# Linear attention and a gated convolution FFN on one core: PSUM handed out in single banks, with a new order

## The chip, the core and the metric

The kernel runs on one core of one Trainium2 chip. Its engines work side by side and wait for each other through semaphores: TensorE (PE in the profile; its weight loads are shown apart as PEld), VectorE (DVE), ScalarE (ACT), GpSimd (POOL, which here issues the loads that cast from fp32 to bf16) and SyncE (SP, which issues the stores). TensorE writes its results to PSUM, an accumulator of 128 partitions and eight banks; a bank holds 512 fp32 numbers per partition. DVE and ACT read PSUM and write SBUF.

The metric is the time of one execution on the device in microseconds (us), median of the runs shown. The kernel before takes 180.43 us (three runs, 179.78 to 180.63).

## The reference

There are 8 batches, 8 heads, 576 tokens and 64 numbers per head; the model width is 8 x 64 = 512, and the FFN is 1024 wide.

```
kv  = einsum('bhsd,bhse->bhde', k, v)          # linear attention, no softmax
out = einsum('bhsd,bhde->bhse', q, kv)
x   = out / sqrt(mean(out*out, -1) + 1e-6) * g_norm      # per head, then heads side by side
h   = maximum(x @ w_in, 0)
c   = conv_w[0]*h[t-1] + conv_w[1]*h[t] + conv_w[2]*h[t+1]
y   = (h * sigmoid(c)) @ w_out                  # float32, 8 x 576 x 512
```

## The kernel before

**An order written out.** The body defines small operations, one Python function each (decorated with `op`). A long string, ORDER, names them one after the other, and the kernel records them in that order; at the end a dependency is added between neighbours of each engine, so every engine executes its own instructions in the order of the string. A token such as `hm.0.4.0@3` means operation `hm` with arguments 0, 4, 0, and the number behind `@` names the buffers that it opens. A letter behind `!` is the engine that does an eviction: A for ACT, V for DVE. Nothing is scheduled at run time: where an instruction waits, all behind it on its engine wait too.

**PSUM before.** All accumulators come from one pool with four tags `a0` to `a3`, each of 1024 fp32 columns, so two banks. `tl` opens a tile in a tag; the next tile in that tag waits until every reader of the last one is done, even if it needs one bank alone.

**The stages**, with the operations that the prediction speaks of:

- Loads: `Lq`, `Lk`, `Lv` load a batch of q, k or v, often in halves (two of the four head groups), into two buffers per tensor; `Li` and `Lo` load the weights. All are on POOL's queue, in the order of the string (L358, L372, L377). A load waits until the batch before the last has been used up. The first halves of batch 0 come through SP instead and are cast by `ca`.
- Attention per batch b and half u: `qt` transposes q (36 small matmuls, L422) and `qc` copies the result to SBUF (qT); `kv` multiplies k by v (36 small matmuls, L397) and `kvc` copies it (kvw); `ot` makes the outputs of two head groups (L443).
- Norm of batches 0 and 1: `sq` squares, `on` sums over each head (L432, L433), `nl` takes the reciprocal root on ACT (L465), and `mz` writes the normed x (xT) on DVE (L472). Of batches 2 to 7, in pairs: `sq`, `oc` (copy of the output to SBUF), `ss` (sums), `ln`, `sl` (four DVE instructions that split the root into two parts, L501 to L504), `sp` (spreads it over the partitions, L513) and `mu` (DVE, L520). `sl.3` belongs to the third pair, batches 6 and 7.
- First projection: for batches 0, 1, 6 and 7 `hm` in two steps of two contractions (L536, 288 columns each) and `re` for the relu. For the pairs of batches (2, 3) and (4, 5), 1152 tokens long, `ha.p.f.e` makes 512 tokens (e = 0, 1) of feature block f (L549); `rea` is their relu, over 1024 columns at once; `hb` and `reb` do the last 128 tokens.
- Convolution and gate: `ta` (two multiplications by a tap, L585 and L586), `aa` and `ab` (sums, L592 and L598) on DVE, `sg` (sigmoid, ACT, L630), `mg` (product of gate and h, DVE, L636).
- Second projection: `om.p.k.i` makes group k of the output tiles of pair p with half i of the eight contraction blocks; a group is two tiles of 128 tokens (two banks) or one. i = 0 and i = 1 are placed on their own, and either may come first. `ea` copies the group to SBUF (a row buffer, one of four), and `st` stores it. The very last tile (3, 6) is done in two halves of 256 columns.
- Fillers: `fi`, `fn`, `fq`, `fo` are matmuls on zeros that nobody reads. They stand in the first 35 us, where PE would have nothing to do.

`sw` ties the next store to a load: the store waits until that load has landed.

The lines that say how a tile of PSUM is opened and how the groups of the second projection are evicted:

Of the kernel before, what the change touches and what calls it, by code (L numbers as in the profile page):

```python
# [66 lines left out]
STORES2 = [(0, 1), (0, 2), (0, 0), (0, 3)]  # L67
# [8 lines left out]
Li.0 mz.0.0 sq.0.2@2 qc.1.0!V@2 fn.2.128.on.0.2@3 on.0.2 sq.0.3@3 nl.0.2@1 mz.0.2 on.0.3@1 nl.0.3 mz.0.3 hm.0.4.0@3
hm.0.5.0@1 hm.0.1.0@2 hm.0.5.1 hm.0.4.1 Li.3 hm.0.1.1 hm.0.0.0@0 re.0.5!A@1 ta.0.5@0 re.0.4!A ta.0.4 hm.0.0.1 aa.0.2
re.0.1!A re.0.0!A Lq.1.1 ab.0.2 qt.1.1@1 hm.0.7.0@3 sg.0.4 Lk.1.0@1 hm.0.6.0@2 Lv.1.0@1 Li.1 ta.0.1@1 hm.0.6.1
re.0.6!A ta.0.0 kv.1.0@0 kvc.1.0!V hm.0.7.1 qc.1.1!V@3 Lv.1.1 ot.1.0@0,2 hm.0.2.0@1 hm.0.2.1 sg.0.5 aa.0.0 re.0.7!A
sq.1.0@4 ab.0.0 sq.1.1@5 sg.0.1 hm.0.3.0@3 re.0.2!V sg.0.0 hm.0.3.1 Lk.1.1 Lq.2.0@0 mg.0.2 re.0.3!V fq.1.512.kv.1.1@1  # L80
kv.1.1 kvc.1.1!V Lk.2.0@0 fo.2.384.1.0 on.1.1@3 nl.1.1@2 ta.0.7@0 on.1.0@1 ta.0.6 mg.0.0 Lv.2.0@0 fo.5.384.1.0
qt.2.0@3 mz.1.1 nl.1.0 qc.2.0!A@4 fq.1.512.ot.1.1@1 fq.1.256.ot.1.1 ot.1.1@2 sq.1.3@6 mz.1.0 Lq.3.1@1 aa.0.3
fo.2.384.1.2 kv.2.0@3 on.1.3@0 Lq.2.1 sq.1.2@7 kvc.2.0!A fo.2.384.1.3 on.1.2@3 nl.1.3@3 nl.1.2 fo.1.384.1.2 hm.1.6.0@0
ab.0.3 hm.1.4.0@3 ta.0.2@1 mz.1.3 mz.1.2 fi.2.512@2 hm.1.4.1 sg.0.7 re.1.4!A hm.1.6.1 Lq.3.0 ta.0.3 qt.2.1@2 re.1.6!A
aa.0.1 Lv.3.1@1 qt.3.0@1 qt.3.1@3 ab.0.1 hm.1.7.0@0 hm.1.7.1 Lk.3.1@1 sg.0.6 Lk.2.1 sg.0.3 qc.3.0!V@0 qc.3.1!V@1
sg.0.2 hm.1.0.0@1 re.1.7!A qc.2.1!V@2 hm.1.0.1 mg.0.3 ta.1.6@0 ta.1.7 ot.2.0@3,2 re.1.0!A oc.2.1@4 sq.2.1@0 Lv.2.1
Lo.0 hm.1.2.0@0 hm.1.2.1 oc.2.0 sq.2.0@1 mg.0.1 aa.1.3 hm.1.5.0@1 hm.1.5.1 re.1.2!A hm.1.3.0@2 hm.1.3.1 re.1.5!A
ta.1.4@1 kv.2.1@3 re.1.3!A kv.3.1@0 ab.1.3 kvc.2.1!V Lo.1 hm.1.1.0@1 ot.2.1@3,2 ta.1.5 sg.1.6 Lk.3.0 kvc.3.1!V sg.1.7
aa.1.2 ab.1.2 oc.2.2@0 hm.1.1.1 sq.2.2@2 Lv.3.0 om.0.1.0@0 re.1.1!V sg.1.5 ot.3.1@3,1 Lq.4.1@0 sq.2.3@3 Lq.5.0@1
mg.1.3 ta.1.0@0 ta.1.1 sg.1.4 oc.2.3 mg.1.2 om.0.1.1 aa.1.0 ta.1.2@1 oc.3.3@1 sq.3.2@5 om.0.0.0@2 sq.3.3@4 kv.3.0@1  # L90
oc.3.2 ab.1.0 ta.1.3 kvc.3.0!V qt.4.1@3 ea.0.1!A@0 aa.1.1 sg.1.1 qc.4.1!V@3 ab.1.1 sg.1.0 mg.1.0 ot.3.0@0,1 om.0.0.1
om.0.2.1@3 ea.0.0!V@1 sq.3.0@6 sq.3.1@7 ss.2@2 ss.3 sg.1.2 sg.1.3 mg.1.1 ln.1@0 Lv.5.1@0 sl.1@0 oc.3.0@2 Lk.5.0@0
# [24 lines left out]
sg.3.4 re.6.0!A sg.3.5 ta.4.6@0 hm.7.0.0@3 hm.6.5.1 re.6.5!A hm.7.0.1 re.7.3!V ta.4.7 hm.7.6.0@1 hm.6.3.0@2 hm.7.6.1
aa.4.3 ab.4.3 st.1.0 hm.6.3.1 hm.7.2.0@0 re.7.6!A mg.3.2 sg.4.7 re.7.0!A hm.7.2.1 re.7.2!A om.2.4.0@1 ta.4.5@1 ta.4.4
aa.4.2 ab.4.2 sg.4.6 hm.7.1.0@3 om.2.4.1 ea.2.4!A@0 sg.4.5 sg.4.4 re.6.3!A mg.4.3 ta.5.7@0 ta.5.6 aa.5.3 ab.5.3 mg.4.2
ta.4.2@1 ta.4.3 aa.4.1 sg.5.6 hm.6.1.0@0 hm.6.1.1 sg.5.7 mg.5.3 ab.4.1 hm.7.1.1 re.6.1!A ta.4.1@0 sg.4.3 ta.4.0  # L120
om.2.0.0@1 om.2.0.1 om.2.1.1@2 om.2.1.0 ea.2.0!A@1 sg.4.2 st.1.1 aa.4.0 ab.4.0 om.2.3.1@0 om.2.2.1@1 sg.4.0 sg.4.1
st.2.0 om.2.3.0 mg.4.1 ea.2.1!A@2 ta.5.4@1 mg.4.0 ta.5.3@0 ta.5.5 aa.5.2 ta.5.2 ab.5.2 om.3.1.0@2 aa.5.1 ea.2.3!A@3
sg.5.5 om.3.0.0@0 om.3.0.1 re.7.1!V om.3.1.1 ab.5.1 sg.5.4 mg.5.2 sg.5.2 st.2.1 st.2.3 ea.3.0!A@1 st.3.0 ta.5.0@1
ea.3.1!A@2 ta.5.1 aa.5.0 ab.5.0 sg.5.0 om.3.2.1@3 om.2.2.0 sg.5.1 mg.5.0 st.3.1 sg.5.3 om.3.5.1@0 om.3.3.1@2
ea.2.2!A@3 st.2.2 mg.5.1 om.3.3.0 om.3.2.0 st.2.4 om.3.4.0@1 ea.3.2!V@1 ea.3.3!A@2 st.3.3 om.3.5.0 ea.3.5!A@3 st.3.2
om.3.6.1@2 st.3.5 ea.3.6.1!A@0 st.3.6.1 om.3.4.1 ea.3.4!A@2 st.3.4 om.3.6.0 ea.3.6.0!A@1 st.3.6.0
"""


@with_exitstack  # L130
def kernel(
    ctx: ExitStack,
    tc: tile.TileContext,
    q: bass.AP,
    k: bass.AP,
    v: bass.AP,
    g_norm: bass.AP,
    moe_w_in: bass.AP,
# [20 lines left out]
    work = pool("work", 1)  # L159
    psum = pool("psum", 1, space=PSUM)  # L160

    T = {}
    ops = {}
    slots = []

    def tl(key, r, shape, dtype, name):
        if key not in T:
            s = slots.pop(0)
            kw = {}
            if r == "a":  # L170
                n = 1
# [115 lines left out]
    def first_tile(name, *a):  # L287
        if name == "ot":
            b, j = a
            return tl(("ot", b, 2 * j if b in JOINT else j), "a", [P, 1024], FP32, "o_ps")  # L290
# [445 lines left out]
```

## Time and profile before

| | us |
|---|---|
| median of three runs | 180.43 (179.78 to 180.63) |
| profiled execution | 180.49 |
| its span, first to last instruction | 178.7 |
| PE busy | 169.0 |
| DVE busy | 151.5 |
| ACT busy | 143.4 |
| POOL busy | 34.7 |
| ACT, output copies (row) of 1024 and 512 columns | 13 of 1.030, 6 of 0.594 |
| ACT, relu of 1024 and 512 columns | 13 of 1.030, 2 of 0.612 |
| DVE, relu of 1024 and 512 columns | 3 of 1.221, 2 of 0.684 |

The last three rows are mean durations of one instruction. Instructions overlap at their ends: a duration is longer than the step from one start to the next. The chain of work that ended last counts such steps, so the prediction takes its prices from there. The profiled execution's own time is 1.8 us longer than its span, for what lies before the first instruction and behind the last. A busy PE need not be a productive one: zeros for nobody count as busy, and matmuls overlap, so columns per time are the better measure.

### The profile page before, as it was taken

Reading aid. Unit: us, or ns where it says so; the run is one execution under the profiler, and the core shown is the slowest. Engines: PE = TensorE matmul, PEld = TensorE weight load, DVE = VectorE, ACT = ScalarE, POOL = GpSimd, SP = SyncE. Lnnn points to the kernel's source line nnn. Section 1 sums busy time; section 2 is a strip of 40 time slices with the busy share of each in tenths; the row PEclk is TensorE's granted clock in tenths of the full one; section 3 lists DMA queues with packets and bytes.
Section 4 is the critical chain, followed back from the end, with each engine's and each line's share of the span. In section 5 each row is a group of like instructions: output and inputs, shape, how many; then the busy total and the mean of one; then the engine's idle time right before and its main releaser. Section 6 shows DMA issues by size and latency. Waiting matters only on the chain.

```text
span 178.7 us, 5121 instructions
## 1 busy us (share of the span) xinstructions
PE 169.0 (95%) x2206; PEld 91.3 (51%) x2206; DVE 151.5 (85%) x271; ACT 143.4 (80%) x200; POOL 34.7 (19%) x60
## 2 busy tenths in 40 slices
PE   7898998999999989989999999999999999999992
PEld 2344754577444454544454474343478764444451
DVE  2467699999997794999999999999999999999410
ACT  2575699999999647979998999999479984757832
POOL 6954536441643022400000000000000000000000
PEclk9999999999999999999999999999999999999999
DMA  5999999999999999999970000001075000242674
GB/s 196 357 200 198 204 207 205 207 205 207 208 206 207 209 226 152 206 185 254 172 269 6 0 6 0 0 4 59 0 274 201 0 0 0 94 189 72 235 293 176
DMA packets 21354, 27.21 MB, mean 152 GB/s; under 512 B 1224, under 2 KB 15828, under 8 KB 21332
## 3 DMA queue, kind: packets, MB, share of 16 engines
q0 software_dynamic: 15072, 15.09, 51.5%
q1 hardware_dynamic: 6256, 11.80, 17.7%
q8 instruction: 17, 0.28, 0.6%
q14 instruction: 5, 0.04, 0.1%
q10 hardware_dynamic: 4, 0.00, 0.0%
HBM read 32.52 MB, written 9.44 MB: 235 GB/s over the span
## 4 chain that ended last, share of the span: by engine, by line
PE 37%; ACT 29%; DVE 21%; DMA 5%; issue 4%; POOL 2%; POOLq 0%; ACTq 0%
PE om_ps L655 22%; PE h_ps L536 10%; ACT taps L630 8%; ACT h L228 7%; DMA q_sb<-in_q_dram 5%; ACT sq L450 5%; ACT o L222 4%; DVE xT L520 3%; DVE taps L585 3%; DVE taps L586 3%; DVE taps L598 2%; DVE taps L592 2%; ACT L217 2%; DVE h L636 2%; DVE h L230 1%
## 5 line engine op out<-in xcount | busy, mean ns | idle before, releaser
L655 PE MATMUL om_ps<-w_out_sb,h 128*128 128x512 bf16 x280 | 63.5, 379 | 0.3 <-DVE xT L520 0.3
L630 ACT ACTIVATE taps<-taps,cw 128x576 bf16<-128x576 bf16 (+1 forms) x48 | 43.9, 956 | 6.4 <-DVE taps L598 6.2
L655 PEld LDWEIGHTS <-h 128*128 128x128 bf16 x280 | 26.6, 98 | 31.9 <-issue 2.1
L536 PE MATMUL h_ps<-xT,w_in_sb 128*128 128x288 bf16 x256 | 33.8, 286 | 0.4 <-ACT o L465 0.2
L228 ACT ACTIVATE h<-h_ps 128x576 bf16<-128x576 f32 (+2 forms) x42 | 30.6, 770 | 3.7 <-PE h_ps L536 3.5
L549 PE MATMUL h_ps<-xT,w_in_sb 128*128 128x512 bf16 x128 | 29.7, 380 | 0.0
L536 PEld LDWEIGHTS <-w_in_sb 128*128 128x128 bf16 x256 | 24.6, 98 | 8.9 <-issue 2.0
L222 ACT ACTIVATE row<-om_ps 128x1024 f32<-128x1024 f32 (+2 forms) x21 | 17.7, 844 | 12.1 <-PE om_ps L655 9.2
L636 DVE TENSOR_TENSOR h<-h,taps 128x1152 bf16<-128x1152 bf16 (+1 forms) x24 | 22.7, 951 | 1.9 <-ACT taps L630 1.8
L598 DVE TENSOR_TENSOR taps<-taps,h 128x1152 bf16<-128x1152 bf16 (+1 forms) x24 | 22.9, 954 | 0.6
L592 DVE TENSOR_TENSOR taps<-taps 128x1152 bf16<-128x1152 bf16 (+1 forms) x24 | 23.0, 956 | 0.4
L450 ACT ACTIVATE sq<-o_ps 128x576 bf16<-128x576 f32 x32 | 20.5, 680 | 2.7 <-PE o_ps L443 2.7
L585 DVE TENSOR_SCALAR taps<-h,cw 128x576 bf16<-128x576 bf16 (+1 forms) x48 | 20.8, 434 | 1.8 <-ACT h L228 1.8
L586 DVE TENSOR_SCALAR taps<-h,cw 128x576 bf16<-128x576 bf16 (+1 forms) x48 | 20.4, 425 | 0.0
L520 DVE SCALAR_TENSOR_TENSOR xT<-o,cw,sp_ps 128x576 bf16<-128x576 f32 x24 | 18.1, 809 | 1.3 <-PE sp_ps L513 1.3
L549 PEld LDWEIGHTS <-w_in_sb 128*128 128x128 bf16 x128 | 11.7, 98 | 14.2 <-issue 1.4
L222 ACT ACTIVATE o<-o_ps 128x576 f32<-128x576 f32 x24 | 15.5, 677 | 1.0 <-ACT o L222 0.8
L358 POOL DMA_DIRECT2D v_sb<-in_v_dram x13 | 9.4, 720 | 18.6 <-PE kv_ps L397 13.3
L358 POOL DMA_DIRECT2D q_sb<-in_q_dram x13 | 9.4, 721 | 14.8 <-PE qt_ps L422 11.0
L217 ACT ACT_TABLE_LOAD x8 | 10.3, 1283 | 2.1 <-issue 2.0
L230 DVE TENSOR_SCALAR h<-h_ps 128x576 bf16<-128x576 f32 (+2 forms) x10 | 8.8, 878 | 2.4 <-PE h_ps L549 2.4
L358 POOL DMA_DIRECT2D k_sb<-in_k_dram x12 | 8.7, 724 | 3.6 <-PE kv_ps L397 1.7
(78 smaller groups left out, 138.2 us busy)
## 6 DMA issues: line engine op xcount, KB each, us to landing
out_dram<-row SPq DMA_DIRECT2D x10, 512.0 KB, 2.8
out_dram<-row SPq DMA_DIRECT2D x15, 256.0 KB, 3.0
q_sb<-in_q_dram POOLq DMA_DIRECT2D x11, 288.0 KB, 11.1
v_sb<-in_v_dram POOLq DMA_DIRECT2D x11, 288.0 KB, 10.9
k_sb<-in_k_dram POOLq DMA_DIRECT2D x10, 288.0 KB, 10.8
stg<-in_k_dram SPq DMA_DIRECT2D x2, 576.0 KB, 6.0
q_sb<-in_q_dram POOLq DMA_DIRECT2D x2, 576.0 KB, 10.2
v_sb<-in_v_dram POOLq DMA_DIRECT2D x2, 576.0 KB, 10.1
```

The costliest lines, as they stand in the source:

```text
L222: nc.scalar.activation(to, fr, AX.Copy)
L228: nc.scalar.activation(to, fr, AX.Relu)
L358: loads[x, b] = nc.gpsimd.dma_start(out=qkv(x, b)[:, w0:w0 + n, :], in_=rows(x, b, w0, n))
L450: nc.scalar.activation(by_r(s), natural(T["ot", b, t][:, :S]), AX.Square)
L536: nc.tensor.matmul(ps[:, e, :HS], w_in_sb[:, t, f * P:(f + 1) * P], x[:, t, e * HS:(e + 1) * HS], start=(t == 0), stop=(t == NT - 1))
L549: nc.tensor.matmul(ps[:, e], w_in_sb[:, t, f * P:(f + 1) * P], x[:, t, e * 512:(e + 1) * 512], start=(t == 0), stop=(t == NT - 1))
L585: nc.vector.tensor_scalar_mul(tap[:, 0, f % 2, :n, 8:8 + S], h[:, f], cw[:, f:f + 1])
L592: nc.vector.tensor_add(tap[:, 1, :, :n, :S], tap[:, 0, :, :n, 7:7 + S], tap[:, 1, :, :n, 1:1 + S])
L598: nc.vector.tensor_add(y, y, h[:, 2 * j:2 * j + 2])
L630: nc.scalar.activation(y, y, AX.Sigmoid, scale=scale)
L636: nc.vector.tensor_mul(h, h, T["tap", c, j][:, 1, :, :n, :S])
L655: nc.tensor.matmul(ps[:, j], h[:, f, m * P:(m + 1) * P], w_out_sb[:, f, :], start=first and f == 4 * i, stop=not first and f == 4 * i + 3)
```

## The change

PSUM becomes one tile of eight banks, and a number in the order is now a bank, 0 to 7. An accumulator that needs two banks takes the named one and its neighbour; one that needs one bank takes that alone. Dependencies follow the columns that are written and read.

Two things are done in smaller pieces. `ha` opens one bank for each 512 tokens, and `rea` has an instruction for each (32 in place of 16). `om` makes one output tile of 128 tokens at a time (a fourth argument j), in a bank of its own, and `ea` copies that tile alone; the store still takes the whole group. The number of matmuls that compute something is the same. The fillers name a bank in place of an accumulator.

The order is new from the second token on. The loads have other places in POOL's queue; some evictions are on another engine than before; the fillers are other ones (36 and 20 of 128 columns in place of nine and six of 512 at the start, for instance). Operations that the order did not use (`cd`, `cp`, `fn`) are gone. STORES2, which says which groups are stored in two pieces, lists the same four in another sequence.

```diff
-STORES2 = [(0, 1), (0, 2), (0, 0), (0, 3)]
+STORES2 = [(0, 0), (0, 3), (0, 2), (0, 1)]
...
-pre@0,0,0 ca.q.1!V ca.q.0!A fi.9.512@1 fi.1.128@1 qt.0.0@0 pn Lq.0.1 ca.k.1!V qc.0.0!A@0 Lv.0.1 ca.k.0!V fi.6.512@2
...
-ea.2.2!A@3 st.2.2 mg.5.1 om.3.3.0 om.3.2.0 st.2.4 om.3.4.0@1 ea.3.2!V@1 ea.3.3!A@2 st.3.3 om.3.5.0 ea.3.5!A@3 st.3.2
-om.3.6.1@2 st.3.5 ea.3.6.1!A@0 st.3.6.1 om.3.4.1 ea.3.4!A@2 st.3.4 om.3.6.0 ea.3.6.0!A@1 st.3.6.0
+pre@0,0,0 Lq.0.1 ca.q.0!V ca.q.1!V fi.36.128@0 fi.3.128@0 qt.0.0@0 qc.0.0!V@0 fi.1.512@2 fi.20.128@2 ct@0 ca.k.1!V
...
+om.3.1.1.0 om.3.0.1.1 ea.3.1.0!V sg.5.1 ea.3.0.1!V sg.5.3 mg.5.1 st.3.1 om.3.3.1@2 om.3.4.1@0 sg.5.0 st.3.0 om.3.2.1@1
+mg.5.0 ea.2.0.1!V st.2.0 om.3.4.0 ea.3.4!A@1 om.3.2.0 om.3.5.0 ea.3.2!V@3 om.3.3.0 st.3.4 st.3.2 ea.3.5!A@2 st.3.5
+ea.3.3!V@0 st.3.3 om.3.6.1@0 ea.3.6.1!V@1 st.3.6.1 om.3.6.0 ea.3.6.0!A@3 st.3.6.0
...
+    banks = psum.tile([P, 8 * 512], FP32, name="banks")
+
     def tl(key, r, shape, dtype, name):
         if key not in T:
             s = slots.pop(0)
-            kw = {}
             if r == "a":
                 n = 1
                 for d in shape[1:]:
                     n *= d
-                cols = 1024 if dtype == FP32 else 2048
-                assert n <= cols
-                kw = dict(padded_shape=[P] + list(shape[1:-1]) + [cols // (n // shape[-1])])
-            T[key] = (psum if r == "a" else work).tile(shape, dtype, name=name, tag=f"{r}{s}", bufs=1, **kw)
+                t = banks[:, s * 512:s * 512 + (n if dtype == FP32 else n // 2)]
+                t = t if dtype == FP32 else t.bitcast(dtype)
+                T[key] = t if len(shape) == 2 else t.rearrange("p (a c) -> p a c", a=shape[1])
+            else:
+                T[key] = work.tile(shape, dtype, name=name, tag=f"{r}{s}", bufs=1)
         return T[key]
...
     @op
     def fi(n, cols):
-        ps = psum.tile([P, 512], FP32, name="fi_ps", tag=f"a{slots.pop(0)}", bufs=1, padded_shape=[P, 1024])
+        s = slots.pop(0)
+        ps = banks[:, s * 512:(s + 1) * 512]
...
-            "ha": lambda p, f, e: tl(("ha", p, f), "a", [P, 2, 512], FP32, "h_ps"),
+            "ha": lambda p, f, e: tl(("ha", p, f, e), "a", [P, 512], FP32, "h_ps"),
             "hb": lambda p, j: tl(("hb", p, j), "a", [P, 4, P], FP32, "h_ps"),
-            "om": lambda p, k, i: tl(
-                ("om", p, k), "a", [P, 2 if (p, k) == HALFOUT else len(OMT[p][k]), D_model], FP32, "om_ps"),
+            "om": lambda p, k, i, j=0: tl(
+                ("om", p, k, j), "a", [P, 2 if (p, k) == HALFOUT else 1, D_model], FP32, "om_ps"),
...
     @op
-    def rea(p, f, eng):
-        relu(eng, flat(h_tile(p))[:, f, :1024].rearrange("p (e n) -> p e n", e=2), T["ha", p, f])
+    def rea(p, f, e, eng):
+        relu(eng, flat(h_tile(p))[:, f, e * 512:(e + 1) * 512], T["ha", p, f, e])
...
-        for j, m in enumerate(ms):
-            for f in range(4 * i, 4 * i + 4):
-                nc.tensor.matmul(
-                    ps[:, j], h[:, f, m * P:(m + 1) * P], w_out_sb[:, f, :],
-                    start=first and f == 4 * i, stop=not first and f == 4 * i + 3)
-
-    @op
-    def ea(p, k, c=None, eng=None):
-        if c is None:
-            copy(eng, tl(("os", p, k), "row", [P, len(OMT[p][k]), D_model], FP32, "row"), T["om", p, k])
+        first = T.setdefault(("om0", p, k, j), i) == i
+        m = ms[j]
+        for f in range(4 * i, 4 * i + 4):
+            nc.tensor.matmul(
+                ps[:, 0], h[:, f, m * P:(m + 1) * P], w_out_sb[:, f, :],
+                start=first and f == 4 * i, stop=not first and f == 4 * i + 3)
+
+    @op
+    def ea(p, k, j=0, eng=None):
+        if (p, k) == HALFOUT:
+            copy(eng, tl(("os", p, k, j), "row", [P, 1, 256], FP32, "row"), T["om", p, k, 0][:, j:j + 1, :256])
         else:
-            copy(eng, tl(("os", p, k, c), "row", [P, 1, 256], FP32, "row"), T["om", p, k][:, c:c + 1, :256])
+            row = tl(("os", p, k), "row", [P, len(OMT[p][k]), D_model], FP32, "row")
+            copy(eng, row[:, j:j + 1], T["om", p, k, j])
```

More of the change, by code (lines that the diff above doesn't have):

```diff
@@ L76 @@
[L76 to L80, printed above, removed]
@@ new lines @@
+fo.1.384.0.1 fq.1.256.1@6 ot.0.1@6,0 sq.0.2@0 mz.0.1 fq.1.512.0@2 qt.1.1@2 Li.1 Lv.1.0@1 fi.2.128@4 on.0.2@4 sq.0.3@7
+nl.0.2@0 qc.1.1!V@0 fo.2.384.0.2 on.0.3@2 nl.0.3 Lk.1.0@1 fo.1.384.0.3 hm.0.5.0@4 mz.0.2 Lq.2.0@0 hm.0.4.0@2 mz.0.3
+hm.0.1.0@6 hm.0.5.1 re.0.5!A@0 hm.0.4.1 ta.0.5@0 hm.0.1.1 re.0.4!A ta.0.4 qt.1.0@0 hm.0.0.0@2 hm.0.0.1 hm.0.3.0@4
+hm.0.3.1 re.0.1!A ta.0.1@1 Lv.1.1 hm.0.6.0@6 qc.1.0!A@1 Lv.2.1@0 re.0.0!A aa.0.2 hm.0.2.0@0 hm.0.2.1 ab.0.2
+fq.1.512.0@2 kv.1.0@2 sg.0.4 ta.0.0 re.0.3!V aa.0.0 Lk.1.1 sg.0.5 ab.0.0 kvc.1.0!A hm.0.6.1 re.0.2!A ot.1.0@4,2
@@ new lines @@
+hm.1.4.1 aa.0.3 mg.0.1 re.1.5!A kv.2.0@6 re.1.4!A Lo.0 hm.1.2.0@0 hm.1.2.1 ab.0.3 sg.0.6 sg.0.7 hm.1.6.0@2 ta.1.5@0
+ta.1.4 Lk.3.1@1 kvc.2.0!V hm.1.6.1 Lo.1 ot.2.0@4,6 re.1.2!A re.1.6!A Lq.3.0 oc.2.1@0 kv.2.1@0 kvc.2.1!A Lq.5.0@0
+hm.1.3.0@2 aa.1.2 mg.0.3 hm.1.3.1 sq.2.1@0 hm.1.0.0@0 hm.1.0.1 ta.1.7@1 sq.2.0@1 oc.2.0 ab.1.2 sg.1.5 om.0.0.0.0@7
+sg.1.4 re.1.3!V ta.1.6 re.1.0!V ot.2.1@5,3 oc.2.3@1 sq.2.3@2 Lq.5.1 kv.3.1@0 om.0.0.0.1@2 aa.1.3 mg.1.2 om.0.0.1.1
+Lk.3.0 sq.2.2@3 oc.2.2 kvc.3.1!V ot.3.1@0,3 ta.1.0@0 Lv.3.0 ea.0.0.1!A@0 ab.1.3 ta.1.1 qt.3.0@5 sg.1.7 sg.1.6
@@ new lines @@
+rea.1.4.1!A sp.4.1.0@4 mu.4.0.0 sp.4.0.1@0 mu.4.1.0 ha.1.7.1@3 sg.2.3 mu.4.0.1 sw.q.6 st.0.4 hb.2.1@2 reb.2.1!V@0
+sg.2.2 ot.7.0@4,6 mg.2.0 Lk.6@1 ta.2.5@1 rea.1.7.1!A oc.7.1@0 ta.2.4 kv.6@0 ha.1.7.0@2 kvc.6!V sq.7.1@0 ha.2.3.0@3
+oc.7.0 ha.2.7.0@6 sq.7.0@1 aa.2.2 ha.1.6.1@7 rea.1.7.0!A ot.7.1@4,0 rea.2.3.0!A rea.1.6.1!V ab.2.2 rea.2.7.0!A
+qt.6.0@2 ha.2.7.1@6 oc.7.2@1 sq.7.3@2 sq.7.2@3 oc.7.3 ha.2.6.0@7 mg.2.1 ta.2.6@0 sg.2.4 qc.6.0!V@0 rea.2.7.1!A
+ha.2.2.0@4 ha.2.1.0@0 ha.2.4.0@1 rea.2.4.0!V ha.2.3.1@5 sg.2.5 ta.2.7 rea.2.6.0!A rea.2.1.0!A rea.2.2.0!A aa.2.3
@@ L287, in first_tile @@
     def first_tile(name, *a):
-        if name == "ot":
-            b, j = a
-            return tl(("ot", b, 2 * j if b in JOINT else j), "a", [P, 1024], FP32, "o_ps")
         return {
@@ L296, in first_tile, with fq @@
             "hm": lambda b, f, u: tl(("hm", b, f), "a", [P, 2, 512], FP32, "h_ps"),
-            "ha": lambda p, f, e: tl(("ha", p, f), "a", [P, 2, 512], FP32, "h_ps"),
+            "ha": lambda p, f, e: tl(("ha", p, f, e), "a", [P, 512], FP32, "h_ps"),
             "hb": lambda p, j: tl(("hb", p, j), "a", [P, 4, P], FP32, "h_ps"),
-            "om": lambda p, k, i: tl(
-                ("om", p, k), "a", [P, 2 if (p, k) == HALFOUT else len(OMT[p][k]), D_model], FP32, "om_ps"),
-            "cp": lambda c, f: tl(("cp", c, f), "a", [P, 1024], FP32, "c_ps"),
+            "om": lambda p, k, i, j=0: tl(
+                ("om", p, k, j), "a", [P, 2 if (p, k) == HALFOUT else 1, D_model], FP32, "om_ps"),
         }[name](*a)
-    def columns(t):
-        return t if len(t.shape) == 2 else t.rearrange("p a c -> p (a c)")
-    @op
-    def fn(n, cols, *a):
-        ps = columns(first_tile(*a))
-        for _ in range(n):
-            nc.tensor.matmul(ps[:, :cols], zero[:, :P], zero[:, :cols], start=True, stop=True)
-    @op
-    def fq(n, cols, *a):
-        ps = columns(first_tile(*a))
-        cross = 0 if a[1] in JOINT else a[-1] % 2
+    @op
+    def fq(n, cols, rows):
+        s = slots.pop(0)
         for _ in range(n):
             for c in range(2):
-                for r in (range(2) if a[0] == "kv" else [c ^ cross]):
-                    at = r * 512 if a[0] == "kv" else 0
-                    nc.tensor.matmul(
-                        ps[half[c], at:at + cols], zero[half[r], :D], zero[half[r], :cols],
-                        start=True, stop=True)
+                r = (0, c, 1 - c, 1)[rows]
+                nc.tensor.matmul(
+                    banks[half[c], s * 512:s * 512 + cols], zero[half[r], :D], zero[half[r], :cols],
+                    start=True, stop=True)
     @op
@@ L327, in fo @@
         for _ in range(n):
-            nc.tensor.matmul(T["ot", b, t][:, S:S + cols], zero[:, :P], zero[:, :cols], start=True, stop=True)
+            nc.tensor.matmul(T["spare", b, t][:, :cols], zero[:, :P], zero[:, :cols], start=True, stop=True)
     @op
@@ L435, in ot @@
     @op
-    def ot(b, i):
-        u, cs = (i, (0, 1)) if b in JOINT else (i // 2, (i % 2,))
-        for c in cs:
-            tl(("ot", b, 2 * u + c), "a", [P, 1024], FP32, "o_ps")
+    def ot(b, u):
+        o = []
+        for c in range(2):
+            s = tl(("ot", b, 2 * u + c), "a", [P, 1024], FP32, "o_ps")
+            T["spare", b, 2 * u + c] = s[:, S:]
+            o.append(s)
         for at in (slice(512, S), slice(0, 512)):
             for v in range(2):
-                for c in cs:
+                for c in range(2):
                     nc.tensor.matmul(
-                        T["ot", b, 2 * u + c][half[v], at], kvw[b % 2][half[c ^ v], 2 * u + v, :],
+                        o[c][half[v], at], kvw[b % 2][half[c ^ v], 2 * u + v, :],
                         T["qT", b, u][half[c ^ v], v, at], start=True, stop=True)
@@ L600, in cd @@
     @op
-    def cd(f, eng):
-        T["dg", f] = consts.tile([P, 2, P], BF16, name=f"dg{f}")
-        for i in range(2):
-            at = 2 * NF * i + f
-            if eng == "A":
-                nc.scalar.activation(T["dg", f][:, i], ident, AX.Copy, scale=cw[:, at:at + 1])
-            else:
-                nc.vector.tensor_scalar_mul(T["dg", f][:, i], ident, cw[:, at:at + 1])
-    @op
-    def cp(c, f):
-        ps = first_tile("cp", c, f)
-        h = span(c)[0][:, f, 0, :]
-        dg = T["dg", f]
-        nc.tensor.matmul(ps[:, 512:S], ident, h[:, 512:S], start=True, stop=False)
-        nc.tensor.matmul(ps[:, 512:S], dg[:, 0], h[:, 511:S - 1], start=False, stop=False)
-        nc.tensor.matmul(ps[:, 512:S - 1], dg[:, 1], h[:, 513:S], start=False, stop=True)
-        nc.tensor.matmul(ps[:, 0:512], ident, h[:, 0:512], start=True, stop=False)
-        nc.tensor.matmul(ps[:, 1:512], dg[:, 0], h[:, 0:511], start=False, stop=False)
-        nc.tensor.matmul(ps[:, 0:512], dg[:, 1], h[:, 1:513], start=False, stop=True)
-    @op
     def sg(c, f):
@@ L625, in sg @@
         scale = cw[:, NF + f:NF + f + 1]
-        if ("cp", c, f) in T:
-            nc.scalar.activation(taps(c, f // 2)[:, 1, f % 2, 0, :S], T["cp", c, f][:, :S], AX.Sigmoid, scale=scale)
-            return
         y = T["tap", c, f // 2][:, 1, f % 2, :CONV[c][1], :S]
@@ L640, in om @@
     @op
-    def om(p, k, i):
+    def om(p, k, i, j=0):
         ms = OMT[p][k]
-        ps = first_tile("om", p, k, i)
-        first = T.setdefault(("om0", p, k), i) == i
+        ps = first_tile("om", p, k, i, j)
         h = flat(T["h", p])
```

95 lines of the change are left out of this document (46 added, 49 removed).

## The prediction

> **What bounds the kernel now.** I read the busy times of the engines first, then the table of busy time by stretch, then the chain that ended last, then TensorE's (PE's) waits, and only then the groups of instructions, for prices.
>
> ```profile
> PE 169.0 (95%) x2206; PEld 91.3 (51%) x2206; DVE 151.5 (85%) x271; ACT 143.4 (80%) x200; POOL 34.7 (19%) x60
> ...
> PEclk9999999999999999999999999999999999999999
> ```
>
> Three engines are above 80%, so an average tells little. The stretches tell more (columns: stretch, length, then busy us and instructions of each engine, granted clock, DMA share, GB/s):
>
> ```profile
> 16.00:35.50 19.50, 18.06 (x301) 11.33 (x302) 17.29 (x35) 17.24 (x25) 9.86 (x14) 1.00 1.24 206
> 35.50:60.00 24.50, 23.84 (x480) 13.76 (x479) 23.03 (x48) 24.46 (x41) 9.28 (x13) 1.00 1.22 207
> 60.00:73.00 13.00, 12.48 (x270) 6.76 (x266) 9.47 (x12) 8.12 (x14) 2.23 (x3) 1.00 1.08 194
> 73.00:120.00 47.00, 45.89 (x592) 22.71 (x593) 46.12 (x62) 44.80 (x60) 2.22 (x3) 1.00 0.46 98
> ...
> 146.00:175.60 29.60, 29.53 (x146) 13.99 (x143) 21.67 (x45) 18.43 (x27) 0.00 (x0) 1.00 0.39 147
> ```
>
> PE has no slack from 35.5 us on, and its work there is real: the last filler of the start (L285) begins at 34.91 us. Before that, PE waits for data or runs fillers. VectorE (DVE) is full too, except from 60 to 73 us; ScalarE (ACT) has room after 120 us. The chain agrees about the end and gives spacings (start us, us, what):
>
> ```profile
> 26.23 0.67 DVE h L230
> ...
> 42.76 1.62 ACT h L228 x3
> ...
> 51.35 0.92 ACT row L222
> ...
> 78.49 1.15 DVE h L230
> ...
> 128.75 13.72 PE h_ps L536 x112
> ...
> 146.15 26.76 PE om_ps L655 x124
> ...
> 175.56 0.38 ACT row L222
> ```
>
> A matmul of 512 columns takes 26.76/124 = 0.216 us of the stream, one of 288 takes 13.72/112 = 0.1225. So PE's work sets the end: 0.86 us for each bank-sized half of an output tile (four matmuls), until 175.53. Then come a 0.38 us eviction, a store, and the end of the span at 178.7; the execution took 180.49, 1.8 more than its span and 0.06 above the median of 180.43.
>
> What can a finer PSUM give? PE's waits after 35.5 us that a held two-bank buffer explains:
>
> ```profile
> PE qt_ps L422 <- DVE h L230: 0.7, 1, 0.7
> ...
> PE sp_ps L513 <- ACT row L222: 0.4, 1, 0.4
> ...
> PE kv_ps L397 <- ACT h L228: 0.3, 1, 0.3
> ```
>
> The 0.7 is batch 7's transposes waiting for a 1024-wide relu on DVE, the 0.4 a spread matmul behind an output eviction, the last 0.3 batch 7's k-v product behind a 1024-wide relu on ACT. Together 1.4 us: that is all that PSUM visibly costs a packed PE.
>
> **The parts, priced.**
>
> *The useful PE work is the same*: 280 + 16 output matmuls, 256 + 128 + 64 of the first projection, and so on. Fillers grow from about 9.6 to 10.5 us by their columns, but all except one of 0.11 us stand before 35 us, where the sums below let DVE set the time. I price them at nothing; should a filler delay what follows, it costs up to the 0.9 us by which they grew.
>
> *Splitting evictions.* Sixteen relus and fourteen output copies of 1024 columns become pairs of 512. On ACT 1024 columns step at 0.92 and 576 at 1.62/3 = 0.54, so 512 is some 0.49 by that slope, and a pair costs 0.05 more than one. On DVE, 1.15 and 0.67 give 0.60, also 0.05 more. Thirty splits are 1.5 us over two engines. They lie beside PE as long as the engine is not late; the bounds are 0 and 1.5, and it belongs in DVE's sum.
>
> *Stage to 35.5 us.* The path to batch 0's last xT slice is as before: v's second half lands at 12.70, then its product, copy, squares, and L472 on DVE, which ends at 18.11. From there DVE is full up to the last xT slice of batch 1, and its list changes by one relu more (+0.67), one qT copy more (+0.70, step of that copy in the chain 0.67), one tap pair fewer (0.37 + 0.28 = -0.65) and two kvw copies fewer (-0.5): +0.2 us, so 35.6 in place of 35.4. PE, which waits for it at L536, has by then done two transpose steps more and one k-v product fewer, 0.48 us each: 0.48 ahead. Gain 0.3.
>
> *Loads.* k of batch 1's second half is now fourteenth on POOL's queue, not twelfth; by the landings of before it arrives at 29.6, and the outputs that need it ran at 30.9. It is covered by 0.4 us after product and copy; without that cover it costs at most the two loads, 2.9 us.
>
> *35.5 to 60 us.* Up to the last gate product of batch 1, DVE does +0.67 (relu), +0.65 (taps), -0.26 (kvw) and one 512 output copy in place of a 1024 (-0.5): +0.5 on 21.4 us. It ends near 57.5 against 56.78, and PE, which waits there for L655's second accumulation, is ahead by one transpose step and one bank half, 0.48 + 0.86 = 1.34. Gain so far 1.34 - 0.7 = 0.6. ACT's list to the same norm is within 0.6 us: two kvw copies more (+0.56), one 512 copy (+0.5), one relu fewer (-0.54).
>
> *60 us to the end, DVE.* Up to the third norm's split (L501, third time), seven 512 relus replace three 1024s and one more 512 and a qT copy leave: 7 x 0.60 - 3 x 1.15 - 0.60 - 0.70 = -0.5. After it DVE has three more output copies and two more relus: 3 x 0.60 + 2 x 0.67 = +3.1. Two of those copies fall where DVE waited before:
>
> ```profile
> 167.61 1.43 DVE L636 TENSOR_TENSOR h<-h,taps 128x1152 bf16<-128x1152 bf16 x2 [1.51 <-ACT taps L630]
> ```
>
> So 3.1 - 1.2 = 1.9 remain, and with 0.2 + 0.5 - 0.5 before it the last gate product moves from 169.04 to about 171.1 if every other idle moment stays. The 3.8 us that DVE idles between 60 and 73 us (its 9.47 busy of 13, and a little) are cover: relus of 512 can start 0.86 us earlier each. I take half of it as used, 1.9, which gives 169.2. PE needs that product with six bank halves left (before: seven), 5.2 us before its end. With PE ending at 174.6 that is 169.4: it just fits.
>
> *The three waits of 1.4 us.* What PE waits for is now half as wide, and the buffer asked for need not be a pair: they vanish (1.4), or come back in new places (0). I take half of it, since an eviction of half the width ends its wait in half the time: 0.7. New small waits, of which the order has many chances (banks come free within tenths of a us of their use between 38 and 56 us): 0.3, between 0 and 1.5.
>
> *The end.* The last eviction now reuses a row buffer whose store is issued some 2.7 us before it, and a store of 256 KB took 3.0 us to landing (median). I take 0.2, between 0 and 0.5.
>
> **Sum.** 180.49 - 0.6 (work moved ahead) - 0.7 (waits halved) + 0.3 (new waits) + 0.2 (end) = 179.7, which is 0.4% under the median. A measurement of this kernel tells about 0.5% from no change, that is 0.9 us.
>
> [...] The first nine fillers start 0.427 us apart and those after 5.9 us 0.216, although the granted clock stands at 1.00 throughout: PE does have a half rate that this row does not show. [...]
>
> **Rivals.**
>
> (a) *PE packs wholly.* Moved work and waits count in full: 180.49 - 0.6 - 1.4 = 178.5, about 178.8 with 0.3 for the end. For it: the stretch rows show nothing else idle. Against: every wait gone and none new.
>
> (b) *DVE becomes the bound* (slower). If the idle of 60 to 73 us returns in full, the last gate product ends at 171.1 and PE 5.2 later at 176.3: 180.49 + 0.8 = 181.3; if the 1.5 us of waiting for the last sigmoids also stays behind the two new copies, 182.5. It decides from the point where DVE's last product is later than 170.3 (175.5 less 5.2). For it: 46.12 busy of 47 from 73 to 120 us. Against: the evictions may land in idle time.
>
> (c) *A late load* (slower). On POOL's queue k of batch 7 now stands ahead of q of batch 7, and waits for batch 5's k-v product, near 67 us. q was first before: issued at 65.39, landed at 73.27, and the next ones landed 2.8 us apart. So q lands at 67.7 + 7.9 + 2.1 = 77.7 or later, and PE wants it near 79. Each us by which that product is later than 68 us is a us of PE: with a third load's 11.8 us to landing 0.5, with 2 us of delay 2: 181 to 182.
>
> (d) *PE falls back to its half rate* once, for as long as at the start: 3.8 us at half rate cost 1.9, so 181.6. The rows give it little: PE's longest wait after 35.5 us is 0.7, and the matmuls behind it kept their spacing. [...]
>
> (e) *One tile for all banks orders all against all*: then every eviction would stop PE. In the built program the waits are by bank (a matmul waits for the last reader of its own bank), so I drop it.
>
> **How the numbers follow.** The forecast's case has 0.38 and reaches from 179.0 to 180.8; some 0.11 of it lies below 179.5. (a) 0.20, (b) 0.24, (c) 0.10, (d) 0.02, and 0.06 that several new waits of 0.3 to 0.5 us add up to more than they save. Faster by over 0.5% (under 179.5): 0.11 + 0.20 = 0.31. Slower by over 0.5% (over 181.3): 0.18 of (b), 0.07 of (c), 0.02 of (d), 0.04 of the last, 0.31. Within 0.5%: 0.38. The range runs from (a) without its 0.3, 178.5, to (b)'s upper end with 0.3 of new waits, 182.8.
>
> **What would show it.** Right: PE's first L536 matmul behind batch 1's last slice near 35.6 us with no filler after it; ACT and DVE rows of 128x512 in place of 128x1024; the last gate product on DVE near 169 and PE's end near 174.6, with no row in PE's waits above 0.5 us after 36 us. Wrong: a filled stretch from 60 to 73 us on DVE and yet a last product after 170.3; q of batch 7 landing after 79; PE's spacing of 512 columns at 0.43 anywhere after 6 us; or a new wait of PE on a one-bank eviction of over 1 us.

## The result and the profile after

The changed kernel takes 185.25 us (median of six runs, 184.39 to 185.84), the kernel before 180.53 beside it (179.78 to 181.10). The ratio is 1.026, with a 95% interval of 1.023 to 1.030: slower by 4.7 us, outside the predicted range of 178.5 to 182.8. The profiled execution took 185.84 us, with a span of 184.0.

The first two parts of the page of the changed kernel (busy times; the clock granted to PE in 40 slices, in tenths):

```profile
PE 172.1 (94%) x2253; PEld 95.4 (52%) x2253; DVE 156.9 (85%) x282; ACT 139.8 (76%) x219; POOL 34.7 (19%) x60
...
PEclk9999999999999965999999999999999999999999
```

Two slices, which lie between 64 and 74 us, show a 6 and a 5 in place of the 9. The table by stretch, with the columns of the prediction (length, then busy us and instructions of PE, PEld, DVE, ACT and POOL, granted clock, DMA share, GB/s):

```profile
16.00:35.50 19.50, 18.59 (x339) 11.93 (x338) 17.61 (x33) 17.07 (x26) 9.94 (x14) 1.00 1.25 205
35.50:60.00 24.50, 24.32 (x479) 13.94 (x478) 23.07 (x49) 24.15 (x43) 9.35 (x14) 1.00 1.22 207
60.00:73.00 13.00, 7.85 (x59) 3.47 (x59) 6.07 (x8) 2.82 (x5) 0.00 (x0) 0.74 0.62 125
73.00:120.00 47.00, 46.69 (x735) 23.60 (x726) 44.40 (x63) 46.26 (x77) 4.47 (x6) 1.00 0.56 117
...
146.00:175.60 29.60, 29.60 (x150) 14.51 (x149) 28.86 (x57) 19.48 (x32) 0.00 (x0) 1.00 0.22 83
```

One stretch stands out. From 60 to 73 us PE is busy for 7.85 of 13 us (12.48 before), DVE for 6.07 (9.47), ACT for 2.82 (8.12) and POOL not at all (2.23), and the clock is 0.74. PE's waits name one culprit, where the kernel before had none above 0.7 us after the start:

```profile
PE banks L628 <- ACT row L232: 5.2, 1, 5.2
```

ACT's own waits from 58 to 68 us say what held ACT:

```profile
ACT row L232 <- DMA out_dram<-row: 5.0, 1, 5.0
```

The chain of work over that stretch (start us, us, what; SPq is SP issuing a transfer) strings it together:

```profile
57.96 0.26 SPq L650
...
58.26 7.65 DMA out_dram<-row
...
66.01 0.61 ACT row L232
...
66.66 1.87 PE banks L628 x4
...
68.88 1.82 PE banks L628 x4
...
71.06 1.81 PE banks L562 x16
```

In words. The new order has `sw.v.5 st.0.0`: the store of output group (0, 0) waits until v of batch 5 has landed (57.77 us). It goes out in two transfers, at 57.85 and 58.26, while six loads are in flight, and the second needs 7.65 us. Its row buffer, number 0, is needed at 61.05 by the copy of output tile (0, 2, 1), written `ea.0.2.1!A@0`. ACT stands there until 66.01. The matmuls of tile (0, 3, 0) want bank 7, which that copy frees, so PE stands from 61.51 to 66.66, and DVE behind PE for 5.64 us. Then comes a second loss: four matmuls of 512 columns take 1.87 us, where the spacing of 0.216 us in the kernel before makes 0.86 and four in e1 below take 1.02; that lasts until 72.8 us.

### The profile page after: what moved, and what is told of

Read it like the earlier page. It is cut to its first block, busy times and chain, and to the rows that moved or that the text cites. A ratio compares the mean times of both kernels' runs of the same rounds, so it can differ in the third digit from the quotient of the medians.

```text
span 184.0 us, 5290 instructions
## 1 busy us (share of the span) xinstructions
PE 172.1 (94%) x2253; PEld 95.4 (52%) x2253; DVE 156.9 (85%) x282; ACT 139.8 (76%) x219; POOL 34.7 (19%) x60
## 4 chain that ended last, share of the span: by engine, by line
PE 61%; ACT 15%; DVE 12%; DMA 8%; issue 2%; SPq 0%; ACTq 0%; DVEq 0%
PE banks L628 25%; PE banks L534 13%; PE banks L547 12%; DMA out_dram<-row 6%; ACT sq L448 4%; ACT taps L603 3%; ACT o L232 3%; DMA stg<-in_q_dram 2%; PE banks L562 2%; ACT h L238 2%; DVE xT L518 2%; PE banks L441 2%; ACT row L232 2%; DVE taps L596 1%; PE banks L393 1%
## 5 line engine op out<-in xcount | busy, mean ns | idle before, releaser
L628 PE MATMUL banks<-w_out_sb,h 128*128 128x512 bf16 x280 | 65.4, 386 | 5.2 <-ACT row L232 5.2
L238 ACT ACTIVATE h<-banks 128x512 bf16<-128x512 f32 (+1 forms) x51 | 29.8, 657 | 6.4 <-PE banks L534 4.2
L534 PE MATMUL banks<-xT,w_in_sb 128*128 128x288 bf16 x256 | 33.5, 286 | 0.4 <-DMA w_in_sb<-in_moe_w_in_dram 0.2
L547 PE MATMUL banks<-xT,w_in_sb 128*128 128x512 bf16 x128 | 30.1, 379 | 0.2 <-ACT row L232 0.2
L232 ACT ACTIVATE row<-banks 128x512 f32<-128x512 f32 (+1 forms) x29 | 16.8, 602 | 16.3 <-PE banks L628 7.2
L534 PEld LDWEIGHTS <-w_in_sb 128*128 128x128 bf16 x256 | 24.5, 98 | 8.4 <-issue 1.1
L518 DVE SCALAR_TENSOR_TENSOR xT<-o,cw,banks 128x576 bf16<-128x576 f32 x24 | 18.2, 808 | 6.7 <-PE banks L511 6.6
L448 ACT ACTIVATE sq<-banks 128x576 bf16<-128x576 f32 x32 | 20.4, 674 | 1.7 <-PE banks L441 1.7
L583 DVE TENSOR_SCALAR taps<-h,cw 128x576 bf16<-128x576 bf16 (+1 forms) x48 | 20.2, 420 | 1.7 <-ACT h L238 1.5
L584 DVE TENSOR_SCALAR taps<-h,cw 128x576 bf16<-128x576 bf16 (+1 forms) x48 | 20.0, 416 | 0.0
L547 PEld LDWEIGHTS <-w_in_sb 128*128 128x128 bf16 x128 | 11.8, 98 | 14.4 <-issue 1.3
L232 ACT ACTIVATE o<-banks 128x576 f32<-128x576 f32 x24 | 15.9, 678 | 0.0
L240 DVE TENSOR_SCALAR h<-banks 128x576 bf16<-128x576 f32 (+1 forms) x17 | 12.2, 719 | 1.1 <-PE banks L547 1.0
```

What stands on the lines that cost most here:

```text
L232: nc.scalar.activation(to, fr, AX.Copy)
L238: nc.scalar.activation(to, fr, AX.Relu)
L448: nc.scalar.activation(by_r(s), natural(T["ot", b, t][:, :S]), AX.Square)
L518: nc.vector.scalar_tensor_tensor(x_tile(b)[:, 2 * tp:2 * tp + 2, at], T["o32", b, tp][:, :, at], g_sb, T["sp", b, tp, e][:, :, :HS], op0=A ...
L534: nc.tensor.matmul(ps[:, e, :HS], w_in_sb[:, t, f * P:(f + 1) * P], x[:, t, e * HS:(e + 1) * HS], start=(t == 0), stop=(t == NT - 1))
L547: nc.tensor.matmul(ps, w_in_sb[:, t, f * P:(f + 1) * P], x[:, t, e * 512:(e + 1) * 512], start=(t == 0), stop=(t == NT - 1))
```

## The experiments

The theory: the wait for the row buffer, and the half rate that follows from the idle time, are the whole loss, and without them the change is faster than the kernel before. The rivals: single banks and split evictions cost by themselves; DVE is the bound; a late load. In the diffs only the tokens that differ are shown.

**Another row buffer** (e1). Row buffer 3 is not used before 88 us, so two tokens swap buffers and nothing else moves.

```diff
-ea.0.2.1!A@0
+ea.0.2.1!A@3
...
-ea.0.4!A@3
+ea.0.4!A@0
```

> The output tiles of group (0, 2) go to row buffer 3, which nothing used before 88 us, and group (0, 4) takes row buffer 0 in its place; all else is the changed kernel. Theory (row buffer): ACT's copy of tile (0, 2, 1) no longer waits 4.96 us for the store of group (0, 0), so PE's wait of 5.15 us and the half rate after it (about 1.8 us more) go: 178.3 to 179.5 us, a ratio to the kernel before of 0.988 to 0.995. The store itself lands as late as it did, near 66 us. Rival 1 (single banks and split evictions cost by themselves): still above 183. Rival 2 (DVE is the bound): 181.3 to 182.5, with the last product of gate and h after 170.3 us. Rival 3 (late load): a wait of 1 to 3 us at the transposes or the second half of batch 7's q, 181 to 182.

Measured: 179.3 us (178.87 to 180.43), ratio 0.9931, interval 0.9910 to 0.9953. The two tokens are worth 5.95 us, and the kernel is now faster than the one before. ACT's timeline (start, duration, operation, in brackets the idle time before it) and PE's around the former stall:

```profile
61.18 1.08 ACT L232 ACTIVATE row<-banks 128x512 f32<-128x512 f32 x2
```

```profile
61.53 0.30 PE L511 MATMUL banks<-wparts,spread 32*128 32x288 bf16 x4
61.83 1.02 PE L628 MATMUL banks<-w_out_sb,h 128*128 128x512 bf16 x4
```

The copy starts at once and PE goes on without a gap. The store is as slow as it was (58.71 to 64.33 and 59.11 to 66.74), but nobody waits for it. The rivals' marks are absent in this run: DVE's last product ends at 168.07 us, below the 170.3 at which rival (b) would decide, and the table by stretch has no hole:

```profile
60.00:73.00 13.00, 12.65 (x240) 6.28 (x235) 11.16 (x20) 9.12 (x17) 2.60 (x4) 1.00 1.02 185
73.00:120.00 47.00, 46.23 (x592) 23.04 (x592) 45.98 (x64) 45.84 (x72) 1.87 (x3) 1.00 0.47 106
```

q of batch 7 lands at 77.43, and PE begins its transposes at 78.50: rival (c) is covered by 1.1 us.

**Fillers in the stall** (e2), to part the wait from the half rate.

```diff
-om.0.3.1.0@7
+fi.22.512@4 om.0.3.1.0@7
```

> The changed kernel with 22 filler matmuls of 512 columns (4.75 us at 0.216) ahead of the matmul that waits for bank 7, in banks that are free by 61.84 us. The wait for the row buffer stays. Theory (row buffer, then a half rate that follows from the idle time): PE is occupied through the wait, the matmuls after it start 0.216 us apart and not 0.43 to 0.47, and the time falls by 1.6 to 2.3 us, to 183.0 to 183.7. If the half rate has another cause (the way the banks are cycled), the spacing stays at 0.43 or more after 66 us and the time at 185 or above.

Measured: 184.67 us (184.53 to 184.76), ratio 1.0218 (1.0196 to 1.0240). PE's timeline:

```profile
62.40 4.91 PE L296 MATMUL banks<-zero 128*128 128x512 bf16 x22 [0.39 <-DVE xT L518]
67.15 1.03 PE L628 MATMUL banks<-w_out_sb,h 128*128 128x512 bf16 x4
```

ACT still waits 4.85 us for the store, but the matmuls behind the fillers run at full rate (1.03 us for four, against 1.87), and the granted clock is 1.00 throughout this execution (0.996 to 1.00 on average in the four). PE's longest idle time from 58 to 76 us is 0.39 us here, against 5.15 in the changed kernel. So in this kernel the half rate came with PE's idle time and not with the way the banks are cycled, since the banks are the same ones. The time missed the 183.0 to 183.7 expected: by medians only 0.6 us are gained on the changed kernel. The loss is at the end and not at the half rate. PE's last group of matmuls (L621) starts 2.06 us earlier than in the changed kernel, as much as the 1.6 to 2.3 that were expected of the whole time. The first line is the changed kernel's, the other two are this run's:

```profile
178.68 1.91 PE L621 MATMUL banks<-w_out_sb,h 128*128 128x256 bf16 x16
```

```profile
176.62 1.91 PE L621 MATMUL banks<-w_out_sb,h 128*128 128x256 bf16 x16
179.62 0.38 ACT L232 ACTIVATE row<-banks 128x256 f32<-128x256 f32 x1 [3.07 <-DMA out_dram<-row]
```

But here the last copy waits for a store once more (issued at 175.82, landed at 179.44). It starts 1.09 us after PE's end, against 0.43 us in the changed kernel, so of the 2.06 us some 1.3 reach the end of the profiled execution.

**The store earlier** (e3).

```diff
-sw.v.5 st.0.0
+st.0.0
```

> The changed kernel without the tie of the first store to the load of v of batch 5: the store of group (0, 0) goes out when its last tile has been copied, near 52.2 us, into the middle of the loads. Theory (row buffer): with 7.7 us to landing it is done near 60, before the copy that needs the row buffer at 61.05, so the waits of 5 us go. Its 512 KB then stand in the way of v of batch 5, of which the product at 59.05 us has 1.3 us to spare after the landing at 57.77; at 207 GB/s 512 KB are 2.5 us, so PE loses between 0 and 1.2 us there: 178.3 to 180.7. If the price of the store falls on the loads in full and more, 181 to 182. If the row buffer is not the cause, 184 or above.

Measured: 179.43 us (179.28 to 179.68), ratio 0.9930 (0.9908 to 0.9953), the same as with the other row buffer. The store goes out at 52.91 and 53.31 and lands at 59.88 and 61.24; ACT's copy starts at 61.66, right behind its predecessor, so the landing has only 0.4 us to spare. The loads hardly mind: v of batch 5 takes 8.5 us to landing, against 8.3 in the changed kernel. It lands at 58.74, and PE, which multiplies by it from 59.77 on, has no wait above 0.2 us after 36 us.

**One transfer in place of two** (e4), that part of the change alone.

```diff
-STORES2 = [(0, 0), (0, 3), (0, 2), (0, 1)]
+STORES2 = [(0, 3), (0, 2), (0, 1)]
```

> The changed kernel with the store of group (0, 0) as one transfer of 512 KB and not two of 256 KB. Theory (the store is slow because loads fill the DMA engines): the bytes and the moment of issue (57.85 us) are the same, so it lands between 65 and 66.5 us and the time stays within 0.5 us of 185.2. If it is the second transfer behind the first that costs, it lands 2 us or more earlier and the time falls by as much, to 183 or less.

Measured: 185.36 us (183.95 to 186.37), ratio 1.0247 (1.0183 to 1.0312). 512 KB in one transfer went out at 58.01 and landed at 66.21, 8.2 us later. The split of the store is not the cause, nor is it that the second transfer stands behind the first.

**A shorter wait** (e6).

```diff
-sw.v.5 st.0.0
+sw.q.4 st.0.0
```

> The changed kernel with the first store tied to the last load of q of batch 4, which landed at 56.35 us, and not to that of v of batch 5 at 57.77: the store goes out 1.4 us earlier. Theory (row buffer): ACT's wait of 4.96 us shrinks by 1.0 to 1.6, PE's of 5.15 likewise, and the time by as much, to 183.6 to 184.3 where the half rate still follows the idle time, and to 182.2 to 183 where 3.7 us of idle are too short for it. If the store's time to landing does not depend on when it goes out, it is 7.7 us again. If the row buffer is not the cause, 185.2.

Measured: 182.53 us (181.25 to 183.50), ratio 1.0111 (1.0073 to 1.0149). The store went out 1.5 us earlier (56.38 and 56.78) and landed 2.0 us earlier (63.87, so 7.1 us later and not 7.7); PE's wait fell to 2.9 us, by 2.2. That is more than the 1.0 to 1.6 expected. The half rate did not go, as the second outcome had it, but got shorter. That the time falls into this outcome's 182.2 to 183 is luck: a wait that shrank more than expected made up for a half rate that stayed. PE's waits, and the table by stretch around the idle time:

```profile
PE banks L628 <- ACT row L232: 2.9, 1, 2.9
```

```profile
61.65:66.00 4.35, 1.42 (x13) 0.56 (x10) 1.89 (x4) 1.08 (x2) 0.00 (x0) 1.00 1.17 231
66.25:69.25 3.00, 3.00 (x22) 1.74 (x21) 2.57 (x4) 0.60 (x1) 0.00 (x0) 0.50 0.25 43
69.50:76.00 6.50, 6.45 (x155) 3.23 (x157) 4.28 (x8) 5.61 (x11) 2.25 (x3) 1.00 0.62 92
```

The four executions sort themselves by mean granted clock: 181.25 us at 0.998, 182.43 and 182.63 at 0.990 and 0.991, 183.50 at 0.981. In the changed kernel five stand at 0.981 (185.17 to 185.84) and one at 0.991 (184.39). So in one and the same kernel the half rate seems to cost 0, 1.3 or 2.3 us, as it happens; only one execution of each kernel has a trace, so that the wait was equally long in the others is not shown.

**The parts alone, in the old order** (e7, e8). First the old kernel with its PSUM as one tile, each old buffer a pair of banks:

```diff
-            T[key] = (psum if r == "a" else work).tile(shape, dtype, name=name, tag=f"{r}{s}", bufs=1, **kw)
+                t = banks[:, s * 1024:(s + 1) * 1024]
...
+            else:
+                T[key] = work.tile(shape, dtype, name=name, tag=f"{r}{s}", bufs=1)
```

> The kernel before with its PSUM as one tile of eight banks, each old buffer a pair of banks at the same place; order and sizes as before. So of the change only the form in which PSUM is handed out, with dependencies by columns. Theory: nothing that waits for a buffer can start earlier, since each pair is written and read whole: 180.2 to 180.9, a ratio of 0.998 to 1.002. Rival (dependencies by bank give or cost time by themselves): more than 0.5 us either way.

Measured: 180.58 us, ratio 1.0002 (0.9985 to 1.0020). Then, on top of it, the split evictions:

```diff
-        relu(eng, flat(h_tile(p))[:, f, :1024].rearrange("p (e n) -> p e n", e=2), T["ha", p, f])
+        for e in range(2):
+            relu(eng, flat(h_tile(p))[:, f, e * 512:(e + 1) * 512], T["ha", p, f][:, e])
...
-            copy(eng, tl(("os", p, k), "row", [P, len(OMT[p][k]), D_model], FP32, "row"), T["om", p, k])
+            row = tl(("os", p, k), "row", [P, len(OMT[p][k]), D_model], FP32, "row")
+            for j in range(len(OMT[p][k])):
+                copy(eng, row[:, j:j + 1], T["om", p, k][:, j:j + 1])
```

> As the run with one PSUM tile and the old order, with every relu and every output copy of 1024 columns split into two of 512, on the same engine and at the same place: 16 relus and 14 copies more. So the split alone, without the new order. By the prediction's 0.05 us for each split 1.5 us of ACT and DVE in all, of which what lies beside PE costs nothing; the first half of a pair of banks is free 0.4 to 0.6 us earlier: between 0.3 us faster and 0.8 us slower than the kernel before, 180.2 to 181.4. Rival (split evictions are what slows the changed kernel): 183 or above. Rival (single banks are the gain of 1.3 us and not the order): 179.3 to 179.8.

Measured: 180.59 us, ratio 1.0009 (0.9993 to 1.0026). By these intervals neither the form of PSUM nor thirty more evictions cost or bring more than 0.3%. The 0.7% that e1 gains belongs to the new order. That order needs single banks, and was not tried without them.

**The end** (e5): e1 with a fifth row buffer for tile (3, 3). In e1 the chain ends through a wait of the same kind:

```profile
168.70 3.84 DMA out_dram<-row
...
172.66 0.52 DVE row L234
...
173.32 0.43 DVE row L234
...
173.94 0.38 ACT row L232
```

```diff
-ea.3.3!V@0
+ea.3.3!V@4
```

> The changed kernel with (0, 2) in row buffer 3 and (0, 4) in row buffer 0, and besides a fifth row buffer for tile (3, 3) alone. In the run with the first edit alone DVE waited 1.75 us for the store of (2, 0) ahead of that tile's copy, at 172.66 us. Theory (the same kind of wait costs at the end too): the wait goes, the last two copies start 0.2 to 0.5 us earlier, and as PE's end at 173.7 us bounds them the time falls by 0.1 to 0.4 us against that run: 178.9 to 179.2, a ratio to the kernel before of 0.989 to 0.993. If the end is set by the stores on SP's queue alone, no difference: 179.3.

Measured: 179.5 us (179.31 to 182.31), ratio 0.9949 (0.9929 to 0.9969): no gain, where 0.1 to 0.4 us were expected. The 1.75 us of DVE are gone, but the next copy waits 0.72 us for its own store. In both runs the last copy starts 0.3 us behind PE's last matmul (0.28 and 0.32): PE's end bounds it in these two. One execution of six took 182.31 us, with a mean granted clock of 0.981 against 0.998 to 1.000 for the other five. There is no trace of that execution, so what dropped the clock there stays open.

## Why the prediction was wrong

**The step that failed** is the term for new small waits, "0.3, between 0 and 1.5". I derived it from banks alone. The order moves another resource as well: a row buffer is free only when its store has landed, and the first store had moved from behind the tie to k of batch 4 (issued at 65.00 us before) to one at 57.85, with its row buffer asked for again 3.2 us later. I looked at row buffers only for the very last eviction ("The end"). The moved store and the reuse of row buffer 0 belonged in the list of moved steps. What it cost: PE's wait of 5.15 us, and the half rate on top. Two of the signs of being wrong that the prediction named came with it: a wait of PE of over 1 us on a one-bank eviction, and 512 columns at 0.43 us or more after 6 us.

**The price would have been wrong too.** In "The end" I used 3.0 us from issue to landing, the median over the stores of 256 KB. With it the store of 58.26 lands at 61.3 and the wait is 0.2 us. But the trace of before has both kinds, by moment of issue. The view of transfers of the kernel before, first for 64 to 66 us, when POOL had issued nothing for 9.5 us up to 65.39, then for 75.5 to 77.5, when POOL had issued three loads since 73.2 (last column: median us to landing):

```profile
out_dram<-row SPq DMA_DIRECT2D x2, 256.0 KB, 2.6
```

```profile
out_dram<-row SPq DMA_DIRECT2D x2, 256.0 KB, 6.4
```

By the second row the store would land at 64.7 us, 3.6 us after it is needed. With 1.9 for the half rate that is 179.7 + 3.6 + 1.9 = 185.2. The prediction's own terms, with this wait among them, come to the measured time; that they meet it so closely is luck, since the wait was 5.15 us and the kernel without it stood 0.4 below 179.7 (179.3 in e1).

**Half rate, rival (d).** It came, where I gave it 0.02. What it came with is one long idle time, as the fillers show: with the same banks and no idle time above 0.39 us (e2, 58 to 76 us) the clock stays at 1.00. That the way the banks are cycled brings it, the other cause that e2 was to tell apart, no run shows. I gave it little because PE's longest wait after 35.5 us was 0.7 us, and with waits of that length the granted clock of the kernel before does stand at 1.00 from there up to PE's end; a wait of 5.15 us was not in my list. Shorter ones had a drop too: the clock fell to 0.50 in e4, 2.5 us into an idle time of 4.8 us, and in e6, behind one of 2.94 us.

**What was right**, read in e1, where the wait is gone. *Work moved ahead* (0.6): in the changed kernel the first L536 matmul (now L534) that needs batch 1's last slice begins at 34.92 us (35.1 in e1), against a predicted 35.6, so the first part of this term was too small by 0.5 to 0.7. *Last gate product*: 168.07, against "near 169". *PE's end*: 173.66, against 174.6. *Waits halved* (0.7 of 1.4, and 0.3 for new ones): all three waits are gone, and what is left of PE's waits from 36 us on are two of 0.2 us, one on ACT (L547) and one on nothing that the profile shows.

*The end* (0.2): the last copy starts 0.28 us behind PE's end, where it was 0.03 before. *Splitting*: no measurable cost in e8, inside the 0 to 1.5. *Rival (c)*: q of batch 7 landing at 77.43, against a worked out 77.7. *Rival (b)*: DVE has 45.98 of 47 us busy from 73 to 120, and neither of these two waits comes from it. *Rival (e)*: rightly dropped, as e7 shows. The numbers of e1 (178.87 in its profiled execution, 179.3 in the median) lie between rival (a), 178.5 to 178.8, and the forecast.

**The account of the 4.7 us**: e1 stands 1.28 below the kernel before (179.30 against 180.58), and the changed kernel stands 5.95 above e1 (185.25), which is what the row buffer costs, wait and half rate together. Sum: -1.3 + 5.95 = 4.7. How the 5.95 divide is best read at PE's last group of matmuls, which starts at 171.75 us in e1, 176.62 in e2 and 178.68 in the changed kernel: 4.9 for the wait and 2.1 for the half rate, in one execution each. These two make 6.9, as the profiled executions lie further apart (178.87 and 185.84) than the medians. By medians e2 would give 5.4 and 0.6, but e2 has a longer wait at its end, which hides part of what the fillers gain.

## What to carry to other kernels

When an order moves a store, write down when its source buffer is wanted again, and compare that with the landing: here the wait for a buffer passed from the store through ACT (5.0 us) to PE (5.2 us), the engine that counts. Price a transfer from rows with the same traffic beside it (the 6.4 us at 76.14 in the kernel before, for the 7.65 us measured here), not from the median over quiet and busy stretches (3.0). And when a change leaves TensorE a new idle time of the length seen here, look for an addition behind it: idle times of 2.94 us (e6), 4.8 (e4) and 5.15 (the changed kernel) came with 3.4, 6.8 and 6.8 us at a granted clock of 0.50. Here fillers took that addition away and left the wait (ACT's 4.85 us in e2); another buffer took both (5.95 us in e1).

## What the runs showed of the hardware

*A store beside loads.* 256 KB issued on SP's queue took 2.3 and 3.0 us near 65 us of the kernel before, when the loads' queue had 39.0% of the DMA engines' time, and 5.5 to 7.9 us among the loads (6.4 in the kernel before at 76.14; 5.5 and 7.7 in the changed kernel, 5.6 and 7.6 in e1, 7.0 and 7.9 in e3, 6.1 and 7.1 in e6); 512 KB in one transfer took 8.2. The queues (packets, MB, share of the time of 16 engines; packets overlap: the second pair of shares adds up to 116.9%) from 65 to 68.5 us of the kernel before, and then from 58.3 to 66 us of the changed kernel; q0 has the loads, q1 the stores:

```profile
q1 hardware_dynamic: 288, 0.52, 42.9%
q0 software_dynamic: 138, 0.14, 39.0%
```

```profile
q0 software_dynamic: 1169, 1.26, 96.3%
q1 hardware_dynamic: 288, 0.52, 20.6%
```

*The drop of the clock.* It is a step to 0.50, and it lasts 6.8 us in the changed kernel (65.9 to 72.7), 6.8 in e4 (64.6 to 71.4) and 3.4 in e6 (66.1 to 69.5). In the changed kernel and in e4 it began while PE was idle, in e6 1.5 us after PE had resumed. From the start of the idle time it came after 4.4 us in the changed kernel, 2.5 in e4 and 4.4 in e6. The table by stretch of the changed kernel, cut at the steps:

```profile
61.50:65.75 4.25, 0.01 (x3) 0.03 (x1) 1.78 (x3) 0.00 (x0) 0.00 (x0) 1.00 1.17 258
66.00:72.50 6.50, 5.84 (x31) 2.56 (x31) 2.93 (x4) 1.68 (x3) 0.00 (x0) 0.50 0.15 25
72.75:76.00 3.25, 3.25 (x100) 1.74 (x98) 1.12 (x3) 2.79 (x6) 1.93 (x3) 1.00 0.16 15
```

Here the granted clock shows the half rate; at the start of the kernel before, with the same spacing (0.427 us from one matmul of 512 columns to the next; one lasts 631 ns here by the median and up to 634 there), the row reads 1.00. So in the kernel before a 1.00 in that row did not mean the full rate. Where the row showed 0.50, the matmuls were slow: the sixteen of 128 columns at L562 took 1.88 us in the changed kernel and 1.87 in e6, against 1.07 in e1 and e2 at 1.00.
